# Rounded copies of the first two head pairs moved from GpSimd to ScalarE, and the last conditional laid out the other way round

## The chip, the cores and the metric

The kernel runs on one core of a Trainium2 chip. TensorE (PE; its weight loads are listed as PEld) multiplies matrices, VectorE (DVE), ScalarE (ACT) and GpSimd (POOL) work on tiles, and SyncE (SP) issues most of the DMA transfers; ACT and POOL issue some too. Every engine runs its own queue of instructions in order and waits on semaphores. The metric is the device time of one execution in microseconds (us); a change is judged against runs of the kernel before on the same chip.

## What is computed

Attention with a threshold, then a mixture of experts, then a second mixture whose experts are causal attentions:

```python
scores = scale * np.matmul(q, k.transpose(0, 1, 3, 2))          # 4 x 8 heads, 576 x 576
thresh = np.max(scores, axis=-1, keepdims=True) - tau
scores = np.where(scores >= thresh, scores, -1000000000.0)
scores = scores - np.max(scores, axis=-1, keepdims=True)
attn = np.exp(scores)
attn = attn / (np.sum(attn, axis=-1, keepdims=True) + 1e-09)
out = np.matmul(attn, v)
...
x = _moe_ref(x=x, **moe_kwargs)          # each token through one of 8 experts
return _moe2_ref(x=x, **moe2_kwargs)     # 4 causal attention experts, top 2 per token
```

## The kernel before

The kernel has three stages. Stage 1 (`stage1`) is the thresholded attention: 32 heads in 16 pairs (p = 0 to 15), each pair in 9 tiles of 128 rows of queries (j = 0 to 8: tiles 0 to 7 alternate between the two heads, a = j mod 2; tile 8 holds the last 64 rows of both). Stage 2 (`moe`) sends tokens through experts, stage 3 (`stage3`) is the second mixture. Almost all work of this change lies in the first 30 us and the last 20 us.

**Accuracy by splitting.** Scores are wanted with more precision than one pass of TensorE on rounded operands gives. So keys and queries are split: a rounded copy (`KK` of the keys times -0.125, `QS` of the queries) and the difference that rounding left (`KL`; for the queries the difference is written over the other 64 partitions of `QS`). `scores` (L242) multiplies `QS` with `KK` and with `KL`.

**Who splits.** `split_k` makes the rounded copy of the keys in two pieces (columns 0 to 575 for head 0, 640 columns for head 1): ScalarE for pair 0 (L191), GpSimd for every later pair (L189). `split_kl` makes the difference: VectorE for pair 0 (L200), GpSimd later (L202 scales the raw keys in place, L203 subtracts). Queries of pairs from 1 on come as a transfer that rounds (`split_q`, issued by GpSimd, L194), and `split_ql` makes the differences (GpSimd, L208). Queries of pair 0 are split by `split_q0` in three pieces of columns `QC` (128, 128 and 320 of each head): a cast (L212) and two subtractions (L215), by VectorE for piece 0 and by GpSimd for pieces 1 and 2. `merge` (L219) and `mixed` (L224, L225) gather operands for tile 8.

**The rest of a tile.** `rowmax` (DVE, L253) takes the extreme of a tile of scores, `thresh` (L258) adds tau, `expo` (ACT, L263) the exponential, `keep` (DVE, L276) applies the threshold; `tp` (PE, L289) transposes, `tp_ev` (ACT, L300, L302) brings the result back to SBUF, `av` (PE, L332) multiplies with the values. The scores rotate through three PSUM buffers (`tag="S", bufs=3`): the scores of a tile start only when `keep` of the tile three before has freed its buffer.

**What sets the order.** The order of stage 1 is written out by hand. `at(g, f, ...)` files a call under a due time g, one unit being a ninth of a pair (tile j of pair p has times 9p + W[name][j]); `E.run()` sorts by due time and then by order of filing, and the instructions go into the engines' queues in that order. Within a queue nothing overtakes.

**The end.** L1806 is a conditional (`tc.If`) around the work for experts whose tokens did not fit into the planned number of columns. It is not entered with these inputs. `preferred_fallthrough_block=False` puts the block for "not entered" straight behind the branch, with the long block "entered" behind it and the closing code (L1873: a barrier of all engines, clearing of semaphores) behind that. The block for "not entered" holds only waits; SP's wait there for the landing of the last transfers.

Of the kernel before, what the change touches and what calls it, by code (L numbers as in the profile page):

```python
# [14 lines left out]
AF = mybir.ActivationFunctionType  # L15
# [24 lines left out]
class Events:  # L40
# [4 lines left out]
    def at(self, g, pri, f, *a):  # L45
        self.n += 1
        self.ev.setdefault(g, []).append((pri, self.n, f, a))
# [67 lines left out]
def stage1(tc, nc, K, qT, qx, kT, vp, tau, wgl, x_dram, L, X, E2, hooks=(), npair=NP):  # L115
# [16 lines left out]
    QS = [E2.tile([128, 2, S], F32R, name=f"QS{i}", tag="w2h", bufs=4) for i in range(NQ)]  # L132
# [19 lines left out]
    Q0, QC = [], (slice(0, 128), slice(128, 256), slice(256, S))  # L152

    def load(p):
        if p:
            qr[p] = P1.tile([128, S], F32, name="qraw", bufs=2)
        kr[p] = P1.tile([128, 1216], F32, name="kraw", bufs=2)
        vr[p] = P1.tile([128, 640], F32, name="v", bufs=2)
        if p == 0:
            Q0.append(P1.tile([128, 2, S], F32, name="q0", tag="P", bufs=5))  # L160
            for i in range(2):
                nc.scalar.dma_start(Q0[0][:, :, QC[i]], qT[p][:, :, QC[i]])
            nc.sync.dma_start(kr[p][:, KC[0]], kT[p][:, KC[0]])
            nc.sync.dma_start(kr[p][:, KC[1]], kT[p][:, KC[1]])
            nc.sync.dma_start(taut, tau)
            nc.sync.dma_start(Q0[0][:, :, QC[2]], qT[p][:, :, QC[2]])
            K.load()
        else:
            nc.sync.dma_start(kr[p], kT[p])
            nc.sync.dma_start(qr[p], qx[p])  # L170
# [12 lines left out]
    def half(a):  # L183
        return slice(64 * a, 64 * a + 64)

    def split_k(p, a):
        o, r = KK[p % NK][:, KC[a]], kr[p][:, KC[a]]
        if p:
            nc.gpsimd.tensor_scalar(o, r, -0.125, 1.0, op0=ALU.mult, op1=ALU.mult)  # L189
        else:  # L190
            nc.scalar.activation(o, r, AF.Copy, scale=-0.125)  # L191
# [17 lines left out]

    def split_q0(k):  # L210
        eng, c = nc.gpsimd if k else nc.vector, QC[k]
        eng.tensor_copy(QS[0][:, :, c], Q0[0][:, :, c])  # L212
        for a in range(2):
            o = QS[0][half(1 - a), a, c]
            eng.tensor_sub(o, Q0[0][half(1 - a), a, c], o.bitcast(F32))  # L215
# [217 lines left out]
    at = lambda g, f, *a: E.at(g, 7, f, *a)  # L433
    for p in range(npair):
        g = 9 * p
        at(g - (27 if p < 2 else 21), load, p)
        at(g - (18 if p < 2 else 4.5), load_v, p)
        if p:
            at(g - (17 if p > 1 else 14.4), split_q, p)
        for a in range(2):  # L440
            if p:
                at(g - 9 + 2 * a, split_k, p, a)
                at(g - 8 + 2 * a, split_kl, p, a)
                at(g - 5 + a, split_ql, p, a)
            else:
                at(2 * a - 7, split_k, p, a)
                at(2 * a - 6, split_kl, p, a)
        if p == 0:
            for k, u in enumerate((-6.5, -5.5, -5.3)):
                at(u, split_q0, k)  # L450
            at(6, prep)
        at(g - 3.5, merge, p)
        if p < NMIX:
            at(g - 1.6, mixed, p)
        for j in range(9):
            for n, f in (("S", scores), ("red", rowmax), ("tau", thresh), ("exp", expo), ("keep", keep), ("tp", tp), ("ev", tp_ev)):
                at(g + W[n][j], f, p, j)
        at(g + W["diag"], diag, p)
        T = W
        if p == npair - 1:  # L460
            T = dict(W, row=(11.3, 14.36), rev=(11.7, 14.7), recip=10.6)
            at(g + 14.72, norm_last)
            at(g + 14.71, logits_last)
            at(g + 14.75, norm_last)
        for h in range(2):
            at(g + T["tpm"][h], tpm, p, h)
            at(g + T["pmev"][h], tpm_ev, p, h)
            for k in range(5):
                at(g + T["av"][h], av, p, h, k)
            at(g + T["xt"][h], av_ev, p, h)  # L470
            at(g + T["row"][h], rows, p, h)
            at(g + T["rev"][h], rows_ev, p, h)
        at(g + T["keep"][8] + 0.1, sums, p)
        at(g + T["recip"], recip, p)
        if p < npair - 1:
            at(g + T["rev"][1] + 0.1, norm, p)
# [14 lines left out]
    for g, f in hooks:  # L491
        g, late = g if isinstance(g, tuple) else (g, None)
# [408 lines left out]
class Weights:  # L901
# [9 lines left out]
    def more(self, pool, *ids):  # L911
        for i in ids:
            self.raw[i] = pool.tile([128, 2048], F32, name=f"raw{i}")
# [782 lines left out]
def model(tc, cst, qT, qx, kT, vp, tau, wgl, w12, wqk, wv, wo, out):  # L1696
    nc = tc.nc
    with ExitStack() as ctx:
# [6 lines left out]
        with ExitStack() as mx, ExitStack() as rx:  # L1705
# [4 lines left out]
            M = Box()  # L1710
# [38 lines left out]
            hooks = [(27, lambda *_: R.clear(tc)), *zip(EARLY, rt.early()), (W0, weights0), (R0, rows0)]  # L1749
            hooks += [*zip(TX0, (tx0(0), tx0(1))), *zip(S0, map(split0, (0, 1, 2, 3, 4, 6)))]  # L1750
            stage1(tc, nc, K, qT, qx, kT, vp, tau, wgl, x_dram, L, X, E, hooks)
            R.more(mx.enter_context(tc.tile_pool(name="mr", bufs=1)), 4, 5)
            W = mx.enter_context(tc.tile_pool(name="mo", bufs=1))
# [27 lines left out]
            def fetch3(b, j, i=None):  # L1781
                xr[b, j] = R.row(i)
                nc.gpsimd.indirect_dma_start(out=xr[b, j], out_offset=None, in_=yg,  # L1783
                                             in_offset=bass.IndirectOffsetOnAxis(ap=rt.slot[:, 4 * j + b:4 * j + b + 1], axis=0))

            def xscale(b, j):
                x = xr[b, j]
                eng = nc.gpsimd if b or j == 4 else nc.vector
                eng.tensor_scalar(x, x, rt.psel[:, 4 * j + b:4 * j + b + 1], 1.0, op0=ALU.mult, op1=ALU.mult)
# [13 lines left out]
        done = stage3(tc, nc, K, ws, xr, fetch3, xscale, R.row, out)  # L1803

        f = 2 * (PMAX + LMAX)
        with tc.If(nc.values_load(M.erow[0:1, f:f + 1], min_val=0, max_val=1) > 0, preferred_fallthrough_block=False):  # L1806
            with ExitStack() as rest, tc.manual_schedule():
                more(tc, nc, K, R, M, yg, rest)
            for j in range(4):
                fetch3(0, j, j)  # L1810
                xscale(0, j)
            stage3(tc, nc, K, ws, xr, fetch3, xscale, R.row, out, done)
# [64 lines left out]
```

## Time and profile before

| | |
|---|---|
| time before, median of 3 runs | 770.5 us (767.13 to 770.83) |
| profiled execution, its own time | 769.05 us |
| its span in the trace | 767.2 us |
| busy PE / DVE / ACT / POOL, share of the span | 95% / 71% / 64% / 38% |
| POOL busy, 20 to 40 us | 18.34 of 20 us |
| last instruction of the program proper (ACT L1626) | starts at 758.24 us |

The 1.85 us between the time and the span lie around the traced program. A profile of one execution gives each instruction a start, a duration and, where its engine stood idle before it, what ended the idle time. "Busy" of PE is modelled from the starts of the matmuls, so gaps under a matmul's length do not show as idle. POOL's shares are an average over three stages: it works mostly in the first.

### The profile page before, as it was taken

What the parts mean: (1) busy time and instruction counts of PE and PEld (TensorE: products, weight loads), DVE (VectorE), ACT (ScalarE), POOL (GpSimd) and SP (SyncE); (2) the same over time, 40 slices, a digit from 0 to 9 for tenths busy, and PEclk for the clock granted to TensorE, in tenths of its full rate; (3) what the DMA queues carried; (4) which work ended last, traced back from release to release, by engine and by line L of the source; (5) the groups of instructions that cost most, each with busy time, mean ns of one, the idle gap of its engine ahead of it and who ended that gap; (6) DMA issues with size and microseconds to landing.
All of it is one profiled execution on the core that took longest, in us unless ns stands there. A gap on an engine that the chain in (4) does not pass through costs nothing.

```text
span 767.2 us, 14238 instructions
## 1 busy us (share of the span) xinstructions
PE 732.3 (95%) x5076; PEld 619.5 (81%) x5076; DVE 547.8 (71%) x1423; ACT 488.4 (64%) x1019; POOL 288.3 (38%) x438
## 2 busy tenths in 40 slices
PE   5899999999998998999999999999989999999994
PEld 4787878887876677897899799989778888888873
DVE  7898998999998888613655465554268888978870
ACT  4788887888886684224554464544245887777872
POOL 6988888788777880300110010000383000000000
PEclk9999999999999899899999999999999999999998
DMA  7449443434341520484556656601241000100112
GB/s 250 150 131 311 138 143 127 158 119 128 113 143 34 237 59 18 131 323 167 203 206 236 231 164 212 241 1 52 93 124 56 2 15 1 42 15 29 42 42 86
DMA packets 37408, 95.40 MB, mean 124 GB/s; under 512 B 4336, under 2 KB 14832, under 8 KB 33232
## 3 DMA queue, kind: packets, MB, share of 16 engines
q1 hardware_dynamic: 30688, 73.49, 28.0%
q0 software_dynamic: 5360, 19.34, 8.0%
q10 hardware_dynamic: 1280, 1.57, 0.7%
q8 instruction: 42, 0.69, 0.4%
q14 instruction: 38, 0.31, 0.1%
HBM read 75.58 MB, written 18.81 MB: 123 GB/s over the span
## 4 chain that ended last, share of the span: by engine, by line
PE 53%; ACT 2%; DVE 2%; POOL 1%; issue 1%; ACTq 0%; POOLq 0%
PE py L1029 15%; PE acc L1004 15%; PE AV L1583 3%; PE X L1532 3%; PE misc L1345 1%; PE S L1462 1%; PE S L1463 1%; PE misc L1347 1%; PE misc L1346 1%; PE misc L1382 1%; PE misc L1384 1%; PE misc L1383 1%; PE misc L1614 1%; PE px L973 1%; PE misc L1613 1%
## 5 line engine op out<-in xcount | busy, mean ns | idle before, releaser
L276 DVE SCALAR_TENSOR_TENSOR P<-S,nm,E 128x576 f32<-128x576 f32 x144 | 116.1, 815 | 9.8 <-ACT E L263 3.8
L253 DVE TENSOR_REDUCE nm<-S 128x1 f32<-128x576 f32 x144 | 106.1, 753 | 19.5 <-PE S L242 18.6
L263 ACT ACTIVATE E<-S,nm 128x576 f32<-128x576 f32 x144 | 104.0, 747 | 9.8 <-DVE nm L253 9.1
L242 PE MATMUL S<-KK,QS 128*128 128x288 f32 x256 | 84.0, 343 | 11.2 <-DVE QS L215 5.7
L289 PE MATMUL X<-cst,P 128*128 128x128 f32 x576 | 86.9, 279 | 1.0 <-ACT PT L300 0.5
L1714 POOL DMA_INDIRECT xg<-x_dram,inv x22 | 22.9, 1042 | 166.9 <-PE px L973 151.0
L289 PEld LDWEIGHTS X<-cst,P 128*128 128x128 f32 x576 | 67.2, 142 | 16.5 <-issue 7.2
L300 ACT ACTIVATE PT<-X 128x512 f32<-128x512 f32 x128 | 75.6, 605 | 5.0 <-PE X L289 2.4
L1004 PE MATMUL acc<-xTh,w1l 128*128 128x256 f32 (+2 forms) x256 | 76.7, 300 | 0.0
L1004 PE MATMUL acc<-xTh,w1h 128*128 128x256 f32 (+2 forms) x256 | 76.6, 299 | 0.0
L1004 PE MATMUL acc<-xTl,w1h 128*128 128x256 f32 (+2 forms) x256 | 76.4, 298 | 0.0
L242 PE MATMUL S<-KL,QS 128*128 128x288 f32 x256 | 73.3, 300 | 0.3 <-DVE KL L200 0.3
L996 DVE SCALAR_TENSOR_TENSOR hTl<-acc,hTh 128x352 fp32r<-128x352 f32 (+2 forms) x52 | 30.0, 576 | 59.8 <-ACT hTh L995 59.8
L332 PE MATMUL Y<-PT,v 128*64 128x320 f32 (+1 forms) x512 | 71.3, 422 | 0.9 <-ACT PT L300 0.7
L1029 PE MATMUL py<-w2h,hTh 128*128 128x512 f32 (+2 forms) x176 | 71.1, 404 | 0.0
L1029 PE MATMUL py<-w2l,hTh 128*128 128x512 f32 (+2 forms) x176 | 69.6, 395 | 0.0
L1029 PE MATMUL py<-w2h,hTl 128*128 128x512 f32 (+2 forms) x176 | 69.3, 394 | 0.0
L995 ACT ACTIVATE hTh<-acc 128x352 fp32r<-128x352 f32 (+2 forms) x52 | 26.5, 509 | 63.3 <-PE acc L1004 63.3
L242 PEld LDWEIGHTS S<-KK,QS 128*128 128x128 f32 x256 | 49.6, 194 | 12.9 <-issue 6.0
L332 PEld LDWEIGHTS Y<-PT,v 128*64 128x64 f32 x512 | 34.5, 139 | 26.4 <-issue 6.8
L1783 POOL DMA_INDIRECT raw<-yg,slot x18 | 17.6, 981 | 95.8 <-DMA yg<-y 62.4
L242 PEld LDWEIGHTS S<-KL,QS 128*128 128x128 f32 x256 | 49.9, 195 | 0.6 <-DVE KL L200 0.6
(381 smaller groups left out, 2001.5 us busy)
## 6 DMA issues: line engine op xcount, KB each, us to landing
raw<-in_w_dram SPq DMA_DIRECT2D x32, 1024.0 KB, 5.4
kraw<-in_kT_dram SPq DMA_DIRECT2D x15, 608.0 KB, 4.1
QS<-in_qT_dram POOLq DMA_DIRECT2D x15, 576.0 KB, 4.0
v<-in_vp_dram SPq DMA_DIRECT2D x16, 320.0 KB, 2.9
yg<-y SPq DMA_DIRECT2D x17, 256.0 KB, 5.5
qraw<-in_qx_dram SPq DMA_DIRECT2D x15, 288.0 KB, 2.9
x_dram<-xr SPq DMA_DIRECT2D x16, 256.0 KB, 2.4
yg<-raw SPq DMA_DIRECT2D x1, 3072.0 KB, 13.0
```

What stands on the lines that cost most here:

```text
L242: nc.tensor.matmul(o, QS[p % NQ][:, a, cs], k[i][:, sl(576 * a)], start=(n == 0), stop=(n == 1))
L253: nc.vector.tensor_reduce(nm[:, 0:1], t[:, :, :288], axis=AX.XY, op=ALU.min)
L263: nc.scalar.activation(e, t[:, :, :288], AF.Exp, scale=-1.0, bias=nm[:, 0:1])
L276: nc.vector.scalar_tensor_tensor(PP[p, c][:, S * a:S * a + S].rearrange("p (h n) -> p h n", h=2), t[:, :, :288], nm[:, 1:2], e, op0=ALU.is ...
L289: nc.tensor.transpose(x[:, 128 * kc:128 * kc + 128], pp[:, o:o + 128], ident)
L300: nc.scalar.activation(PT[p, h][:, a, :, f:f + 128], x.rearrange("p (k q) -> p k q", k=4), AF.Copy)
L332: nc.tensor.matmul(out, l, r, start=s, stop=e, skip_group_check=True)
L995: nc.scalar.activation(hh, p, AF.Relu)
L996: nc.vector.scalar_tensor_tensor(hl, p, 0.0, hh.bitcast(F32), op0=ALU.max, op1=ALU.subtract)
L1004: nc.tensor.matmul(o, a[:, fs], x[:, k, 0:w], start=(first and n == 0), stop=(k == 3 and n == 2), skip_group_check=True)
L1029: nc.tensor.matmul(ys[t][u][0:m], h, w[:, 512 * f:512 * f + 512], start=(i == 0 and f == 0 and n == 0), stop=(i == 3 and f == 1 and n == 2))
L1532: nc.tensor.transpose(x[:, 128 * k:128 * k + 128], e[:, 128 * k:128 * k + 128], ident)
```

## The change

Nothing of the arithmetic changes, only who does it and when.

- Queries of pair 0: for pieces 1 and 2 the cast of `split_q0` moves from GpSimd to ScalarE; GpSimd keeps the two subtractions. Piece 1 is due at -4.5 (was -5.5), piece 2 at 0.95 (was -5.3), which is between the exponentials of tiles 0 and 1 in ScalarE's queue.
- The transfer of piece 1 of these queries is issued by SP behind the two of the keys, no longer by ScalarE.
- Keys of pair 1: the rounded copies (`split_k`) move from GpSimd to ScalarE, due 3.45 and 4.05: in its queue behind the exponentials of tiles 2 and 3. The differences follow at 3.5 and 4.1, so that GpSimd's order for pair 1 becomes: keys 0, queries 0, keys 1, queries 1 (it was keys 0, keys 1, queries 0, queries 1).
- `merge` and `mixed` of pair 0 are due at 1.2 and 1.3 (were -3.5 and -1.6), behind GpSimd's issue of `split_q(2)` (due 1.0).
- The last conditional gets `preferred_fallthrough_block=True`: the block "entered" comes straight behind the branch, the block for "not entered" behind it, next to the closing code.

```diff
             Q0.append(P1.tile([128, 2, S], F32, name="q0", tag="P", bufs=5))
-            for i in range(2):
-                nc.scalar.dma_start(Q0[0][:, :, QC[i]], qT[p][:, :, QC[i]])
+            nc.scalar.dma_start(Q0[0][:, :, QC[0]], qT[p][:, :, QC[0]])
             nc.sync.dma_start(kr[p][:, KC[0]], kT[p][:, KC[0]])
             nc.sync.dma_start(kr[p][:, KC[1]], kT[p][:, KC[1]])
+            nc.sync.dma_start(Q0[0][:, :, QC[1]], qT[p][:, :, QC[1]])
...
         o, r = KK[p % NK][:, KC[a]], kr[p][:, KC[a]]
-        if p:
+        if p > 1:
             nc.gpsimd.tensor_scalar(o, r, -0.125, 1.0, op0=ALU.mult, op1=ALU.mult)
         else:
             nc.scalar.activation(o, r, AF.Copy, scale=-0.125)
...
-        eng.tensor_copy(QS[0][:, :, c], Q0[0][:, :, c])
+        if k:
+            nc.scalar.activation(QS[0][:, :, c], Q0[0][:, :, c], AF.Copy)
+        else:
+            eng.tensor_copy(QS[0][:, :, c], Q0[0][:, :, c])
...
-            at(g - (17 if p > 1 else 14.4), split_q, p)
+            at(g - (17 if p > 1 else 13.4), split_q, p)
         for a in range(2):
             if p:
-                at(g - 9 + 2 * a, split_k, p, a)
-                at(g - 8 + 2 * a, split_kl, p, a)
+                at(g - 9 + 2 * a if p > 1 else 3.45 + 0.6 * a, split_k, p, a)
+                at(g - 8 + 2 * a if p > 1 else 3.5 + 0.6 * a, split_kl, p, a)
...
-            for k, u in enumerate((-6.5, -5.5, -5.3)):
+            for k, u in enumerate((-6.5, -4.5, 0.95)):
                 at(u, split_q0, k)
             at(6, prep)
-        at(g - 3.5, merge, p)
+        at(g - 3.5 if p else 1.2, merge, p)
         if p < NMIX:
-            at(g - 1.6, mixed, p)
+            at(g - 1.6 if p else 1.3, mixed, p)
...
-        with tc.If(nc.values_load(M.erow[0:1, f:f + 1], min_val=0, max_val=1) > 0, preferred_fallthrough_block=False):
+        with tc.If(nc.values_load(M.erow[0:1, f:f + 1], min_val=0, max_val=1) > 0, preferred_fallthrough_block=True):
```

## Rows read from the trace of the kernel before

**Rows 1.** Busy time by stretch: PE, PEld, DVE, ACT, POOL; PE's clock; DMA.

```profile
20.00:40.00 20.00, 17.91 (x141) 14.63 (x140) 16.52 (x43) 14.86 (x29) 18.34 (x32) 1.00 0.47 146
...
200.00:220.00 20.00, 20.00 (x162) 17.09 (x161) 18.16 (x47) 17.13 (x34) 13.39 (x21) 1.00 0.48 156
```

**Rows 2.** PE in order of time: start, duration, line, tiles, [idle before, releaser].

```profile
22.39 0.40 PE L242 MATMUL S<-KK,QS 128*128 128x288 f32 x1 [1.63 <-POOL QS L208]
...
23.87 0.40 PE L242 MATMUL S<-KK,QS 128*128 128x288 f32 x1 [0.46 <-POOL QS L208]
```

**Rows 3.** POOL in order of time, columns as in rows 2.

```profile
6.19 1.35 POOL L212 CAST QS<-q 128x256 fp32r<-128x256 f32 x1 [4.85 <-DMA q<-in_qT_dram]
...
9.34 0.72 POOL L212 CAST QS<-q 128x640 fp32r<-128x640 f32 x1
10.15 1.80 POOL L215 TENSOR_TENSOR QS<-q,QS 64x320 fp32r<-64x320 f32 x2
...
14.11 0.68 POOL L189 TENSOR_SCALAR KK<-kraw 128x576 fp32r<-128x576 f32 x1
...
15.63 1.43 POOL L203 TENSOR_TENSOR KL<-kraw,KK 128x576 fp32r<-128x576 f32 x1
16.99 0.59 POOL L194 DMA_DIRECT2D QS<-in_qT_dram  x1
17.61 0.74 POOL L189 TENSOR_SCALAR KK<-kraw 128x640 fp32r<-128x640 f32 x1
...
20.92 2.90 POOL L208 TENSOR_TENSOR QS<-qraw,QS 64x576 fp32r<-64x576 f32 x2
```

**Rows 4.** ACT in order of time, columns as in rows 2.

```profile
5.19 0.74 ACT L191 ACTIVATE KK<-kraw 128x640 fp32r<-128x640 f32 x1 [0.85 <-DMA kraw<-in_kT_dram]
8.52 0.74 ACT L263 ACTIVATE E<-S,nm 128x576 f32<-128x576 f32 x1 [2.59 <-DVE nm L253]
...
12.31 0.74 ACT L263 ACTIVATE E<-S,nm 128x576 f32<-128x576 f32 x1 [2.09 <-DVE nm L253]
13.94 0.60 ACT L300 ACTIVATE PT<-X 128x512 f32<-128x512 f32 x1 [0.89 <-PE X L289]
14.44 1.37 ACT L263 ACTIVATE E<-S,nm 128x576 f32<-128x576 f32 x2
```

**Rows 5.** DVE in order of time, columns as in rows 2.

```profile
15.95 0.81 DVE L276 SCALAR_TENSOR_TENSOR P<-S,nm,E 128x576 f32<-128x576 f32 x1
...
24.70 0.76 DVE L253 TENSOR_REDUCE nm<-S 128x1 f32<-128x576 f32 x1 [0.72 <-PE S L242]
```

**Rows 6.** SP's issues of transfers in order of time, columns as in rows 2.

```profile
3.58 0.43 SPq L173 DMA_DIRECT2D v<-in_vp_dram  x1
5.00 0.57 SPq L175 DMA_DIRECT2D iq<-in_wgl_dram  x1
```

**Rows 7.** Two transfers issued at 6.27 and 8.38: size, us from issue to landing.

```profile
kraw<-in_kT_dram SPq DMA_DIRECT2D x1, 608.0 KB, 5.9
...
qraw<-in_qx_dram SPq DMA_DIRECT2D x1, 288.0 KB, 9.0
```

**Rows 8.** Line L1806, the conditional: count, ns min/median/max, first and last start.

```profile
L1806 SPq EVENT_SEMAPHORE  x9: 17/17/17, 748.2 to 762.5; - x9
...
L1806 SPq COMPARE_BRANCH  x2: 38/48/57, 748.1 to 762.6; - x2
...
L1806 PEldq COMPARE_BRANCH  x2: 95/2157/4219, 754.8 to 757.9; - x2
...
L1806 ACTq COMPARE_BRANCH  x2: 38/43/48, 759.8 to 760.0; - x2
```

**Rows 9.** Line L1873, the closing code, columns as in rows 8.

```profile
L1873 SPq EVENT_SEMAPHORE  x14: 17/28/28, 765.5 to 767.1; - x14
...
L1873 ACTq DRAIN  x2: 8/46/83, 762.6 to 766.6; - x2
```

**Rows 10.** Busy time and clock in a stretch at half clock, columns as in rows 1.

```profile
250.00:253.00 3.00, 2.31 (x10) 1.00 (x10) 2.79 (x13) 1.86 (x3) 2.75 (x3) 0.51 0.00 0
```

## The prediction

> **What bounds the kernel now.** I read the busy time by stretch first. In stage 1's steady part PE is busy for all of 20 us (200 to 220), DVE for 18.2 and POOL for 13.4; between 20 and 40 us PE lacks 2.1 us and POOL has 18.3 [rows 1]. So what PE loses while the pipeline fills is lost for good, for nothing later has room to catch up, and what it gains there stays. PE's order of time then shows where it stands before the first scores of pair 1: 1.63 us at 22.39 and 0.46 us at 23.87, both until POOL's query differences [rows 2]. POOL's order of time shows why: from 6.19 on it works almost without a gap, and what PE waits for comes last, from 20.92 on, two instructions of 1.45 us [rows 3]. At the other end I read the two lines of the conditional and of the closing code. SP's last wait for a landing is over at 762.5, it branches at 762.6, and its next instruction starts at 765.5: 2.9 us after a branch that itself takes 38 ns [rows 8, 9]. ACT shows the same, branch at 760.0 and closing code at 762.6, and for PE the branch at 757.9 is itself recorded with 4.22 us. The first branch of each engine, which is not taken, is followed at once (SP: branch at 748.1, first wait at 748.2) [rows 8]. A taken jump over the long block thus costs 2.6 to 4.2 us, and SP pays it last, when everybody waits for it.
>
> **The front, step by step (times of the trace before in brackets).** POOL loses two casts, 1.35 and 0.72 us, and two copies of keys, 0.68 and 0.74: 3.5 us [rows 3]. ACT gains four copies. The copies of 640 columns and of 576 cost what ACT pays for pair 0, 0.74 and about 0.68 [rows 4]; 256 columns lie between nothing and those 0.74; I take 0.4, in proportion with a fixed part.
> - Query piece 1: it lands at about 6.2 as before (POOL's wait for it ends at 6.19 [rows 3]); ACT is free (its copy of keys ends at 5.93 [rows 4]), so POOL's subtractions start near 6.65 [7.64], a gain of 1.0 for the transfer of pair 1's queries that POOL issues behind them.
> - Query piece 2: ACT copies it behind the first exponential (8.52 + 0.74 [rows 4]) until 10.0. POOL's two subtractions start as before at 10.1 [10.15] and end at 11.9. The second exponential is queued behind the copy, starts near 10.05 and ends 0.1 us after VectorE is ready for it: 0.1 us, which the wait for the fourth exponential takes up again.
> - POOL then issues the transfer of pair 2's queries (0.59 us [rows 3]; was at 16.99), which pushes merge and mixed by 0.6 to an end at 14.7; tile 8 reads them after 19 us, so that is free. The transfer now goes out at 12 beside those of pair 2's keys, which POOL reads only after 25 us: free too.
> - Key differences of pair 1, head 0: from 14.7, as long as before (14.79 to 17.06, 2.3 us [rows 3]) until about 16.9. Query differences of head 0 follow at once, 1.45 us, until 18.3 [22.37]; keys of head 1 (18.35 to 20.92 before, 2.6 us) until 20.9; query differences of head 1 until 22.3 [23.82].
> - What it costs: ACT's copy of key piece 0 sits in the idle 0.89 us between the third exponential (ends 13.05) and the next work at 13.94 [rows 4], so it is free as long as the keys are there by 13.0. They were issued at 6.27 and took 5.9 us, 12.2 [rows 7]. SP now also issues query piece 1 (ACT took some 0.65 us for it), but SP stands idle from 4.01 to 5.00 [rows 6], so that later issues don't move. Copy of piece 1 has no such gap: it stands between the fourth and the fifth exponential (14.44, two in 1.37 [rows 4]) and delays the fifth by 0.74; DVE's keep of that tile (15.95 [rows 5]) slips to 16.6, and since DVE has no idle from there to the end of pair 0's last maximum, all of pair 0 slips by 0.67.
> - Result: PE's last transposes of pair 0 end at 21.4 instead of 20.76 (22.39 - 1.63 [rows 2]). The scores of pair 1 no longer wait for POOL but come at about 21.5 [22.39] and, when DVE has freed the buffer, at 22.65 [23.87]: PE is 1.2 us ahead. DVE gets the second tile at 23.95 [24.70, after 0.72 idle, rows 5], 0.75 ahead; it has enough slack in pair 1 to follow PE. **Front: -1.2 us**, carried to the end because PE is full. Bounds: -2.1 (both waits for POOL gone, nothing lost to the 0.67) and +0.7 (the slip, and no wait removed).
>
> **The end.** With the block for "not entered" next to the closing code each engine jumps at its first branch: SP at 748.1, 14 us before its last landing at 762.5; PE at 754.8, so at 759.1 with the 4.22 us of its own row; ACT at 759.8, 2.6 us, 762.4, hardly earlier than now (762.6) [rows 8, 9]. SP falls from its last wait (762.5) into the closing code, which takes 765.5 to 767.2 as before. **End: -2.9 us**; what is late next is ACT, at 762.5, and it has 0.8 us in hand, for SP runs through a dozen waits before the barrier. Bounds: 0 (a second jump remains) and -2.9.
>
> **The sum.** 769.05 of the profiled execution (span 767.2, 1.85 around it) - 1.2 - 2.9 = 764.95. That execution lies 1.45 under the median of the three runs; the spread is 767.13 to 770.83. I take the middle between the two, 769.8, as the base: 765.7.
>
> **The rivals.**
> - *The keys come late.* ACT's copy of key piece 0 waits at the head of its queue, and behind it the transposes' eviction and the exponential that VectorE needs. Every microsecond of landing after 13.0 costs one. For it: the transfer of pair 1's queries now starts 1 us earlier and shares the DMA engines with the keys. Against: 12.2 leaves 0.8. At 14.2 the front is worth nothing: 769.8 - 2.9 = 766.9.
> - *The same, to the other side.* If the keys' issue is also held up (transfers wait for older ones: SP stood until 5.00) and the landing takes 9 us as the slowest neighbour did [rows 7], 8.0 + 9 = 17 eats all 4.1; from a landing of 17.1 on the kernel is slower, at 18 by 0.9: 770.7. Against: 3 us of issue delay are nowhere in sight.
> - *The jump stays.* The block for "not entered" may still end in a jump for which SP waits 2.9 us, or SP's early jump is undone by something else last: only the front is left, 768.6. For it: it ends in a jump now. Against: its target then stands right behind it. [...]
> [...]
>
> **How the numbers follow.** Forecast 0.62, late keys 0.16, late keys and slower 0.05, jump stays 0.08, a clock stretch less 0.07, one more 0.02. A measurement of this kernel tells about 0.5% (3.85 us) from no change, and the forecast of 4.1 lies close to that: two thirds of its 0.62 count as faster (0.41), the rest as same. Faster 0.41 + 0.07 = 0.48; same 0.21 + 0.16 + 0.08 + 0.02 = 0.47; slower 0.05. The range 763.0 to 769.2 holds the forecast with the spread of the runs, the late keys and the stubborn jump, and leaves out the clock's gift and the slower case.
>
> **What would show it.** Right: ACT copies near 6.2, 9.3, 13.1 and 15.1; no L212 and L189 of POOL before 25 us; PE's waits for POOL L208 gone and the second scores of pair 1 near 22.7; the pause of 2.6 to 4.2 us behind each engine's first branch, and SP's closing code 0.1 us behind its last landing. Wrong: ACT standing for a DMA at 13; PE still standing before pair 1; a pause between SP's last landing and L1873; later pairs of tiles less far ahead than pair 1, which would mean that PE did not bound the fill.

## The result and the profile after

The changed kernel takes 762.53 us (median of five, 762.1 to 763.7) against 770.5 us (767.13 to 771.67). The ratio is 0.9912 [0.9894, 0.9931]: 6.8 us less, with an interval of 5.3 to 8.2. (The two medians lie 8.0 us apart; gains in this document go by the ratios and their intervals.) The forecast was 765.7, 4.1 us less than its base, and the range began at 763.0; the measured median lies half a microsecond below it, and 770.5 x 0.9912 = 763.7 lies inside. The sign and the two places were right, and each place gave more than it was priced at. The profiled execution of after took 762.1 us, span 760.3.

| | before | after |
|---|---|---|
| first scores of pair 0 (PE), us | 5.71 | 4.84 |
| first scores of pair 1 (PE), us | 22.39 | 20.71 |
| first rows of pair 0 evicted (ACT, line 344, now 347), us | 27.46 | 25.44 |
| from ACT's last output transfer to SP's last wait, us | 3.65 | 3.15 |
| from SP's last wait to SP's closing code, us | 2.98 | 0.07 |

**The front.** Here are PE, ACT, POOL and DVE of after in order of time (lines past the edit have moved by 3):

```profile
20.71 0.37 PE L245 MATMUL S<-KK,QS 128*128 128x288 f32 x1
...
21.88 0.37 PE L245 MATMUL S<-KK,QS 128*128 128x288 f32 x1 [0.18 <-DVE P L279]
```
```profile
5.91 0.40 ACT L213 ACTIVATE QS<-q 128x256 fp32r<-128x256 f32 x1
...
8.29 0.73 ACT L213 ACTIVATE QS<-q 128x640 fp32r<-128x640 f32 x1
...
12.30 0.67 ACT L191 ACTIVATE KK<-kraw 128x576 fp32r<-128x576 f32 x1
...
14.42 0.74 ACT L191 ACTIVATE KK<-kraw 128x640 fp32r<-128x640 f32 x1
...
25.44 0.38 ACT L347 ACTIVATE XT<-Y 128x256 f32<-128x256 f32 x1 [0.45 <-PE Y L335]
```
```profile
15.89 1.44 POOL L208 TENSOR_TENSOR QS<-qraw,QS 64x576 fp32r<-64x576 f32 x1
...
19.75 1.42 POOL L208 TENSOR_TENSOR QS<-qraw,QS 64x576 fp32r<-64x576 f32 x1
```
```profile
4.08 0.29 DVE L215 CAST QS<-q 128x256 fp32r<-128x256 f32 x1 [1.88 <-DMA q<-in_qT_dram]
...
14.56 0.82 DVE L279 SCALAR_TENSOR_TENSOR P<-S,nm,E 128x576 f32<-128x576 f32 x1 [0.38 <-ACT E L266]
...
15.82 0.82 DVE L279 SCALAR_TENSOR_TENSOR P<-S,nm,E 128x576 f32<-128x576 f32 x1 [0.43 <-ACT E L266]
```

POOL's last query difference ends at 21.17 [rows 3: 23.82], and PE's waits for it, 1.63 and 0.46 us [rows 2], are gone; the second scores of pair 1 now wait 0.18 us for DVE. ACT's four copies are there at the durations expected, and none of them waits for a transfer. DVE's cast at 4.08 shows one thing that was not expected: the first queries land 0.87 us earlier than in the profiled execution of before, so pair 0 starts earlier by as much.

**The middle.** Between 28 us and the end of the second stage the lead over before grows from 2.0 to 3.3 us, in one place: the half-clock stretch of before [rows 10] is missing. The window of after, then that of the same front with before's closing layout (e2 below):

```profile
250.00:253.00 3.00, 3.00 (x24) 1.81 (x19) 2.94 (x11) 1.04 (x2) 2.85 (x3) 1.00 0.37 85
```
```profile
250.00:253.00 3.00, 3.00 (x14) 1.36 (x13) 2.93 (x12) 0.42 (x1) 2.81 (x2) 0.55 0.28 44
```

**The end.** The conditional and the closing code of after (count, ns min/median/max, first and last start):

```profile
L1809 SPq EVENT_SEMAPHORE  x9: 17/17/17, 747.8 to 758.6; - x9
...
L1809 SPq COMPARE_BRANCH  x1: 53/53/53, 744.8 to 744.8; - x1
...
L1809 PEldq COMPARE_BRANCH  x1: 3482/3482/3482, 751.4 to 751.4; - x1
...
L1809 ACTq COMPARE_BRANCH  x1: 54/54/54, 756.4 to 756.4; - x1
```
```profile
L1876 SPq EVENT_SEMAPHORE  x14: 17/28/28, 758.7 to 760.2; - x14
...
L1876 ACTq DRAIN  x2: 8/8/8, 759.2 to 759.8; - x2
```

Each engine now branches once. SP pays its jump at 744.8 (next instruction at 747.8) while the outputs are still being made, and goes from its last wait (758.6) into the closing code (758.7); before, 2.9 us lay between [rows 8, 9].

### The profile page after: what moved, and what is told of

Same layout as the page of the kernel before. It is cut to its first block, busy times and chain, and to the rows that moved or that the text cites. A ratio compares the mean times of both kernels' runs of the same rounds, so it can differ in the third digit from the quotient of the medians.

```text
span 760.3 us, 14234 instructions
## 1 busy us (share of the span) xinstructions
PE 730.5 (96%) x5076; PEld 618.5 (81%) x5076; DVE 546.9 (72%) x1423; ACT 490.7 (65%) x1023; POOL 284.8 (37%) x434
## 4 chain that ended last, share of the span: by engine, by line
PE 54%; DVE 2%; ACT 2%; POOL 1%; issue 1%; ACTq 0%; POOLq 0%
PE py L1032 15%; PE acc L1007 15%; PE AV L1586 3%; PE X L1535 3%; PE misc L1348 1%; PE S L1465 1%; PE S L1466 1%; PE misc L1350 1%; PE misc L1349 1%; PE misc L1385 1%; PE misc L1387 1%; PE misc L1386 1%; PE misc L1617 1%; PE px L976 1%; PE misc L1616 1%
## 5 line engine op out<-in xcount | busy, mean ns | idle before, releaser
L335 PE MATMUL Y<-PT,v 128*64 128x320 f32 (+1 forms) x512 | 69.1, 412 | 0.9 <-ACT PT L303 0.7
L998 ACT ACTIVATE hTh<-acc 128x352 fp32r<-128x352 f32 (+2 forms) x52 | 26.5, 509 | 63.3 <-PE acc L1007 63.3
```

The lines of the kernel that those rows point to most:

```text
L335: nc.tensor.matmul(out, l, r, start=s, stop=e, skip_group_check=True)
L998: nc.scalar.activation(hh, p, AF.Relu)
```

## The experiments

Each ratio is against the kernel before, measured beside it on the same chip. The table holds what the traces show at the two disputed places. "Rows" is ScalarE's first eviction of pair 0's rows, the last column the time from ACT's last output transfer to the end of the span.

| kernel | ratio and interval | PE's waits for POOL before pair 1's first, second scores | rows | PE's clock, 24 to 26, 26 to 28 us | transfer to end |
|---|---|---|---|---|---|
| before | | 1.63, 0.46 | 27.46 | 1.00, 1.00 | 8.3 |
| after | 0.9912 [0.9894, 0.9931] | none | 25.44 | 1.00, 1.00 | 4.8 |
| e1 layout only | 0.9955 [0.9937, 0.9973] | 2.22, 0.49 | 30.04 | 0.72, 0.50 | 4.8 |
| e2 front only | 0.9957 [0.9941, 0.9972] | none | 25.97 | 1.00, 1.00 | 8.4 |
| e3 one transfer | 0.9980 [0.9962, 0.9999] | 2.13, 0.48 | 29.71 | 0.50, 0.50 | 8.7 |
| e4 transfer put back | 0.9909 [0.9875, 0.9942] | none | 25.96 | 1.00, 1.00 | 4.9 |
| e5 keys only | 0.9908 [0.9877, 0.9939] | none | 25.40 | 1.00, 1.00 | 4.8 |
| e6 queries only | 0.9957 [0.9939, 0.9975] | none, 1.79 | 26.65 | 1.00, 1.00 | 4.9 |
| e7 later copy | 0.9913 [0.9896, 0.9931] | none, 0.25 | 25.14 | 1.00, 1.00 | 4.9 |
| e8 no block | 0.9891 [0.9870, 0.9911] | none | 25.15 | 1.00, 1.00 | 2.9 |
| f1 filled wait | 0.9974 [0.9962, 0.9986] | 0.42, 0.48 | 28.40 | 1.00, 1.00 | 8.2 |
| f2 wait put back | 0.9941 [0.9921, 0.9962] | 2.80, none | 28.27 | 1.00, 1.00 | 5.1 |
| f3 put back, filled | 0.9938 [0.9914, 0.9963] | 0.70, none | 28.19 | 1.00, 1.00 | 5.0 |
| f4 layout, filled wait | 0.9941 [0.9918, 0.9965] | none, 0.49 | 26.96 | 1.00, 1.00 | 5.0 |

**Which part brings what.** e1 takes the kernel before with the new layout alone, e2 the changed kernel with the old layout.

```diff
-preferred_fallthrough_block=False
+preferred_fallthrough_block=True
```

> The kernel before with the conditional laid out the other way round and nothing else. Theory A (the jump is worth its 2.9 us and the last landing was held up besides, by the code that PE loads at that time): the span ends 3.4 us earlier counted from the last ScalarE instruction, some 766.5 us against 770. Theory B (only the jump, the 0.5 us of the last landing are chance): 2.9 us, and the last transfer takes 3.6 us to land as before. In both the front shows pair 1's second scores at 23.9 us as before. Rival (the end gains nothing, all came from elsewhere): time as before.

> The changed kernel with the conditional as before: only the front. Expected: pair 1's second scores at 21.9 us as in the changed kernel (before 23.9), a gain of 2.0 us that holds through stage 1, SP's 2.9 us between its last landing and the closing code back. Time: 2.0 us under before if the rest of the changed kernel's gain (1.2 us lost or won between 245 and 260 us, where PE ran at half clock before and did not after) is chance; 3.3 us under before in every run if the front's shift itself does away with that stretch. The granted clock of the runs tells: 0.986 with it, 0.992 without, in the runs of the changed kernel.

The layout is worth 0.45% (3.5 us), the front 0.43% (3.3 us), and 0.9955 x 0.9957 = 0.9912: the parts add up. In e1's trace the time from the last transfer to the end is 3.5 us shorter than in before (4.8 against 8.3): 2.9 of it is the jump, 0.5 the last landing (3.12 against 3.65 us), as in theory A; its reason, the code that PE loads, is not tested by this run. Its front missed what was expected: pair 1's second scores come at 24.89, not at 23.9; why stands below. e2 gains the 3.3 us and not the 2.0, and yet the half-clock stretch at 250 us stands in its trace, so neither of its two cases holds as it was put; its second scores come at 22.41, not at 21.9, for its first queries land as late as before's. The end was forecast at 2.9 and the front at 1.2, so most of what is missing from the forecast is missing from the front.

e8 is the changed kernel without the block for "not entered".

> The changed kernel without the conditional and its block at the end, so that no engine jumps (the work for experts whose tokens don't fit is left out; it is not entered with these inputs). If the jump is hidden in the changed kernel (every engine's jump ends before SP's last landing or within what SP still does), the closing code starts no earlier after the last landing and the time is the changed kernel's less at most 0.1 us. If ScalarE's jump still counts, up to 0.6 us less. If code loads slow the last landing, it takes 2.7 us or less instead of 3.1.

It is 0.9891, some 1.6 us under the changed kernel, though the intervals overlap. Its trace ends 1.9 us sooner after the last transfer (2.9 against 4.8). The transfer is seen 2.0 us after its issue (755.78 to 757.82) instead of 3.15, and SP's part of the closing code behind that takes 0.9 us instead of 1.6 (compare the row of after's L1876 above):

```profile
L1867 SPq EVENT_SEMAPHORE  x12: 17/28/28, 745.1 to 758.7; - x12
```

So what the conditional still costs in this trace is 1.1 us in the last landing and 0.8 in the closing code; the expectation had at most 0.6 us of time and a landing of 2.7 or less.

**Was it the transfer?** The first queries land 0.87 us earlier in after, and the change takes the transfer of piece 1 off ACT's queue. e3 moves only that transfer in the kernel before; e4 puts it back in the changed one.

```diff
-            for i in range(2):
-                nc.scalar.dma_start(Q0[0][:, :, QC[i]], qT[p][:, :, QC[i]])
+            nc.scalar.dma_start(Q0[0][:, :, QC[0]], qT[p][:, :, QC[0]])
...
+            nc.sync.dma_start(Q0[0][:, :, QC[1]], qT[p][:, :, QC[1]])
```

> The kernel before, with only the transfer of query piece 1 moved from ScalarE's queue to SP's, behind the keys. Theory: behind piece 0 in the same queue it holds up the landing of piece 0 by 0.87 us; so the first scores come at 4.84 instead of 5.71 us, but GpSimd's chain still sets the start of pair 1, and only its own earlier start (piece 1 lands a little earlier) is left there: second scores of pair 1 0.2 to 0.5 us earlier than 23.87, time 0.2 to 0.5 us under before. Rival (the landing was early by chance, or by another part of the change): first scores at 5.71.

> The changed kernel with that one transfer put back into ScalarE's queue. Theory: first scores back at 5.7 us, all of pair 0 0.87 us later, second scores of pair 1 at 22.7 us: this is what the forecast had (22.65), and the front is worth 1.2 us against before instead of 2.0. Rival: first scores stay at 4.84, and the front at 2.0.

In the changed kernel the transfer's new place is not needed: e4 is as fast, within an interval of 0.3% to either side. In the kernel before it may help: e3 is 0.20% faster, 1.5 us [0.1, 2.9], where 0.2 to 0.5 us were expected. The landing of piece 0 scatters by itself. With piece 1 behind piece 0 on ACT's queue VectorE's first cast starts at 4.95 (before), 4.82 (e4), and 4.04 in e1, whose front is that of before, instruction for instruction:

```profile
4.04 0.29 DVE L212 CAST QS<-q 128x256 fp32r<-128x256 f32 x1 [1.85 <-DMA q<-in_qT_dram]
```

With piece 1 on SP's queue it starts at 4.08 (after), 4.21 (e3), 4.83 (e2). So the 0.87 us by which the first queries land earlier in after than in before is chance.

Piece 1 scatters too. Behind piece 0 on ACT's queue the wait for it ends at 6.19 (before), 6.00 (e4) and 5.57 (f4), but at 8.23 in e1 and 8.07 in f1, both with before's front. Here is POOL in e1, its first cast and its last query differences:

```profile
8.23 0.40 POOL L212 CAST QS<-q 128x256 fp32r<-128x256 f32 x1 [6.90 <-DMA q<-in_qT_dram]
...
21.93 2.90 POOL L208 TENSOR_TENSOR QS<-qraw,QS 64x576 fp32r<-64x576 f32 x2
```

POOL's chain then ends at 24.83 and 24.76 instead of 23.82 [rows 3], and pair 1's scores come up to 1.0 us later than in the trace of before. On SP's queue the piece was there by 5.99 in all nine traces. How often it is late on ACT's queue, and whether e3's gain is this, no run shows.

**Which copies?** e5 leaves the casts of pair 0's queries on POOL, e6 the copies of pair 1's keys.

```diff
-        if k:
-            nc.scalar.activation(QS[0][:, :, c], Q0[0][:, :, c], AF.Copy)
-        else:
-            eng.tensor_copy(QS[0][:, :, c], Q0[0][:, :, c])
+        eng.tensor_copy(QS[0][:, :, c], Q0[0][:, :, c])
```
```diff
-        if p > 1:
+        if p:
             nc.gpsimd.tensor_scalar(o, r, -0.125, 1.0, op0=ALU.mult, op1=ALU.mult)
```

> The changed kernel with the casts of pair 0's queries left on GpSimd (cast and two subtractions, at the new places): only the keys' copies and the transfer have moved. GpSimd's chain is 0.7 us longer than in the changed kernel, second query differences ready near 22.0 us instead of 21.2, just when VectorE frees the buffer: second scores of pair 1 at 21.9 to 22.1, time as the changed kernel within 0.2 us. Theory: the queries' copies are worth next to nothing by themselves. Rival: they carry the front, and 1 us or more is lost.

> The changed kernel with the keys' rounded copies of pair 1 left on GpSimd (at the new places): GpSimd's chain is 1.6 us longer, second query differences ready near 22.8 us, while VectorE is 0.67 us earlier for want of the copy before the fifth exponential. Second scores of pair 1 at 22.8 instead of 21.9, time 0.8 us over the changed kernel. Rival (the copies are worth nothing, since what GpSimd saves ScalarE loses): 21.9 and no difference.

The key copies are the whole front that these runs can tell: e5 equals the changed kernel, and e6, which keeps the transfer, the new order of POOL and the query copies, equals e1. In e6 PE still stands 1.79 us for POOL, before the second scores of pair 1:

```profile
23.05 0.40 PE L245 MATMUL S<-KK,QS 128*128 128x288 f32 x1 [1.79 <-POOL QS L208]
```

e6 was expected 0.8 us over the changed kernel and lies 3.8 us over e5 (0.9957 against 0.9908, in the same set of runs). Its trace shows 1.25 of that at the rows (26.65 against 25.40); another 2.0 come behind 244 us (span 763.3 against 760.0), with the half-clock stretch at 250 us, which e5's trace lacks.

e7 gives ACT the copy of the second key piece after the fifth exponential, so that it no longer delays that exponential; POOL's work that needs the copy is filed behind it.

```diff
-at(g - 9 + 2 * a if p > 1 else 3.45 + 0.6 * a, split_k, p, a)
+at(g - 9 + 2 * a if p > 1 else (3.45, 5.53)[a], split_k, p, a)
...
```

> The changed kernel with ScalarE's copy of the second key piece moved from between the exponentials of tiles 3 and 4 to behind the eviction of tile 1, where ScalarE stands idle for 1.1 us before the exponential of tile 5; GpSimd's second key difference and what follows it are filed behind it, in the same order. If the copy in front of the fifth exponential cost pair 0 what the forecast said (0.67 us on VectorE and with it on PE), the second scores of pair 1 come at 21.2 instead of 21.9 us and the kernel is 0.6 us faster than the changed one. Rival: GpSimd is late next and nothing moves (second scores at 21.9).

In its trace the rows come 0.3 us earlier than in after, though its first queries landed 0.35 us later; the second scores come at 21.56, not at 21.2, behind 0.25 us of waiting for POOL. Its time is the same: a gain of that size isn't seen in five runs.

**Why the front is worth 3.3 us.** The traces of e1 and e3 hold a part of the answer. POOL's work before pair 1 is that of before in both, and yet their rows come 2.6 and 2.2 us later than in the trace of before:

```profile
25.03 1.95 PE L332 MATMUL Y<-PT,v 128*64 128x256 f32 x16
```
```profile
27.46 0.38 ACT L344 ACTIVATE XT<-Y 128x256 f32<-128x256 f32 x1 [0.46 <-PE Y L332]
```

In e1 1.0 us of this is POOL's late start; in e3 POOL's chain even ends 0.7 us earlier (23.09). But PE waits longer than the 1.63 us of before (e1, then e3; start, duration, [wait]), and behind the wait its clock is halved:

```profile
23.38 0.40 PE L242 MATMUL S<-KK,QS 128*128 128x288 f32 x1 [2.22 <-POOL QS L208]
...
27.00 2.56 PE L332 MATMUL Y<-PT,v 128*64 128x256 f32 x16
```
```profile
21.64 0.40 PE L242 MATMUL S<-KK,QS 128*128 128x288 f32 x1 [2.13 <-POOL QS L208]
...
25.25 3.68 PE L332 MATMUL Y<-PT,v 128*64 128x256 f32 x16
```

Windows of e1, then e3 (columns as in rows 1):

```profile
24.00:26.00 2.00, 1.51 (x8) 1.27 (x7) 0.76 (x1) 1.02 (x2) 2.00 (x7) 0.72 0.46 172
26.00:28.00 2.00, 2.00 (x11) 1.27 (x12) 1.56 (x3) 0.89 (x2) 1.96 (x6) 0.50 0.44 134
```
```profile
24.00:26.00 2.00, 2.00 (x10) 1.44 (x11) 1.30 (x3) 0.64 (x2) 1.96 (x7) 0.50 0.58 148
26.00:28.00 2.00, 2.00 (x12) 1.08 (x10) 1.78 (x7) 1.22 (x2) 1.69 (x6) 0.50 0.05 12
```

The 16 matmuls that take 1.95 us in before and after take 2.56 and 3.68. From PE's first scores of pair 1 to the rows it is 5.07 us in before (27.46 - 22.39), 6.66 in e1 and 8.07 in e3: 1.6 and 3.0 us go to the clock. The profiled execution of before did not have this stretch: its clock stands at 1.00 from 22 to 30 us. To see what it costs on the mean, f1 gives PE twelve matmuls to do while it stands there, and changes nothing else; f4 is f1 with the new layout.

```diff
         t = PS.tile([128, 2, 512], F32, name="S", tag="S", bufs=3)
+        if (p, j) == (1, 0):
+            for n in range(12):
+                nc.tensor.matmul(t[:, 0, :288], QS[0][:, 0, 0:128], KK[0][:, 0:288], start=True, stop=True)
```

> The kernel before, with twelve more matmuls in front of the first scores of pair 1 (pair 0's operands, into the same accumulator, which the real scores then overwrite): 12 x 0.13 = 1.6 us of work for PE while it stands there for POOL; nothing else is changed. Theory 'the wait brings the half clock': behind the longer of these waits (2.1 and 2.2 us in the two runs with this front) PE ran at 0.50 for 4 to 6 us, and 2.0 us were lost; with PE at work no stretch below 1.00 stands in 20 to 30 us, the first eviction of pair 0's rows (ScalarE, line 344 in the kernel before) lies at 26.5 to 27.5 and not near 29.8, and the time is on the mean 1 to 2 us under the kernel before (ratio 0.9975 to 0.9985). Rival 'the stretch comes by chance, whatever PE does': it still appears in most runs, ratio 1.000. Rival 'the dummies delay the real scores': ratio 1.001 or more, the first scores of pair 1 later than POOL's last query difference by more than 0.1 us.

> The kernel before with the conditional laid out the other way round and with the twelve added matmuls ahead of the first scores of pair 1; copies, order and transfers of the front as before. If the gain of the whole change is the end (3.5 us in the traces with this layout), plus a half-clock stretch that PE's wait in the front brings in most executions (2.0 us by the run with the added matmuls alone), plus some 1.4 us by which pair 1's scores come earlier, then this kernel holds the first two: ratio 0.9955 x 0.9974 = 0.993 (764.9 on 770.3), 1.4 us over the changed kernel (0.9912), and its runs scatter less than those of the kernel before. Rival 'the copies on ScalarE bring all of the front, the clock nothing': as with the layout alone, 0.9955. Rival 'the added matmuls already bring all of the front': 0.9912.

f1 is 0.26% [0.14, 0.38] faster than before, 2.0 us, though PE does more and no data comes earlier. Its trace (the added matmuls; the scores behind them; the rows; a window):

```profile
21.04 1.85 PE L234 MATMUL S<-KK,QS 128*128 128x288 f32 x12
...
23.31 0.40 PE L245 MATMUL S<-KK,QS 128*128 128x288 f32 x1 [0.42 <-POOL QS L208]
...
25.97 1.95 PE L335 MATMUL Y<-PT,v 128*64 128x256 f32 x16
```
```profile
26.00:28.00 2.00, 2.00 (x21) 1.32 (x20) 1.70 (x6) 1.86 (x3) 1.96 (x6) 1.00 0.42 133
```

The clock stands at 1.00. The rows come at 28.40, outside the 26.5 to 27.5 expected, because query piece 1 landed late (POOL began at 8.07); from the first scores to the rows it is 5.09 us, as in before. Over all runs the mean granted clock is 0.9874 in f1 (12 runs) and 0.9846 in the 18 runs of before beside them; the difference, over 767 us, is 2.1 us of PE's time by estimate. The times spread over 2.2 us (766.92 to 769.12) instead of 4.7 (767.53 to 772.25). That is what one stretch less in most executions would look like. The front alone agrees (e2, 0.9881 in 7 runs against 0.9847 in 12), but the mean clock of a few runs is not sharp: e1, with before's front, has 0.9865 in 6. f4 came out at 0.9941: the forecast product of 0.993 lies inside its interval, but so does e1's 0.9955, so it adds little; that the added matmuls bring all of the front is just outside (0.9912 against 0.9918). That its runs would scatter less came true: 3.1 us against 5.0, at a mean clock of 0.9907 against 0.9847.

The other direction failed. f2 puts a wait back into the changed kernel by making POOL late, f3 fills that wait.

```diff
     def split_ql(p, a):
         i = p % NQ
+        if (p, a) == (1, 0):
+            for _ in range(3):
+                r = kr[p][:, KC[0]]
+                nc.gpsimd.tensor_scalar(r, r, 1.0, 1.0, op0=ALU.mult, op1=ALU.mult)
...
-at(g - 5 + a, split_ql, p, a)
+at(g - 5 + a if (p, a) != (1, 0) else 5.05, split_ql, p, a)
```

> The changed kernel with the wait of PE put back: POOL works pair 1's second head first and then scales a slice of the keys that are used up by 1.0 three times (3 x 0.76 us) before it makes the query differences of the first head, so the first scores of pair 1 come near 23.4 instead of 20.7 and PE stands about 2.8 us before them. ScalarE's copies, the transfers and the end stay. Theory 'the wait brings the half clock': PE at 0.50 for some 5 us behind the wait, the 16 matmuls of the rows (128x256) take about 3.7 us instead of 1.95, pair 1 starts 2.0 to 2.7 us later by the wait and 2 us more by the clock: 4 to 5 us over the changed kernel, about 767. Rival 'a wait costs only itself': 2.0 to 2.7 us over it, about 765, clock 1.00.

> The kernel with POOL's query differences put late, and with sixteen more matmuls (2.1 us, pair 0's operands) for PE while it waits for them, as the only difference between the two. Theory 'the wait brings the half clock': PEclk 1.00 through 20 to 30 us, the 16 matmuls of the rows at 1.95 us, 2 us faster than the same kernel without the added matmuls: about 765, 2.0 to 2.7 us over the changed kernel. Rival 'a wait costs only itself': the same time as without them.

PE stands 2.80 us in f2, longer than in e1 and e3, and the clock does not fall behind it:

```profile
23.92 0.40 PE L249 MATMUL S<-KK,QS 128*128 128x288 f32 x1 [2.80 <-POOL QS L212]
...
25.85 1.95 PE L339 MATMUL Y<-PT,v 128*64 128x256 f32 x16
```
```profile
26.00:28.00 2.00, 2.00 (x20) 1.19 (x18) 1.70 (x6) 1.82 (x4) 1.87 (x5) 1.00 0.33 121
```

f2 and f3 take the same time (0.9941, 0.9938), as the rival has it, but with five and four runs and intervals of 0.2% to either side the 2 us in question could hide there. So f2's trace refutes that a long enough wait always halves the clock; how often one does behind this wait is not shown. f2 lies 0.29%, 2.2 us, over the changed kernel, which is what the wait itself would cost. What stays is narrower: behind this wait the clock fell in two of the three traces that hold before's front unfilled (before, e1, e3), and filling the wait made the kernel 2.0 us faster. That these 2.0 us are the clock's is borne out by the mean clock and the spread of the runs, not by a trace of before with and without the stretch. What else decides whether it falls is open.

## Why the prediction came out as it did

- **What bounds the kernel was read rightly.** What PE lost in the fill was lost for good: the lead that after has at its first rows (2.02 us) is still 2.1 at 244 us. Nothing gave it back.
- **The durations held.** 0.4 for the 256 columns (measured 0.40), 0.74 and 0.68 for the others (0.73, 0.67, 0.74). The slip by the copy of key piece 1 was set at 0.67: DVE's keep of the tile before starts 0.65 earlier than in before (14.56 against 15.21), this one 0.13 (15.82 against 15.95 [rows 5]), so it slipped by 0.52. Key pieces came in time (copy at 12.30 without a wait), and both rivals of late keys did not happen.
- **The chain of the front was sized about rightly, at 1.2 us.** Traces whose first queries landed as late as before's are e2 and e4 (first scores at 5.59 and 5.58 against 5.71). Their rows come 1.5 us earlier, 1.4 without those 0.12. Of the 2.02 in the trace of after, the other 0.5 goes with its earlier landing (rows at 25.44 against 25.97 and 25.96).
- **The step that failed is the base of the front.** That PE loses 1.63 and 0.46 us was read from one execution, and its lower bound of -2.1, both waits gone, was taken as the most that there was to gain. In two other traces of the same POOL work the wait was followed by half clock, at 1.6 and 3.0 us. Measured, the front is worth 3.3 us [2.2, 4.5]; 1.4 of it is the chain, and the 1.9 that are left agree with the 2.0 [1.1, 2.9] of f1. That all of the 1.9 is the clock is not shown: the late landing of query piece 1, up to 1.0 us in e1 and f1, is another loss of before's front that its profiled execution was spared. The prediction gave a clock stretch less a chance of 0.07 and one more 0.02 (the trace of before has one at 250 us [rows 10]); it did not ask whether the very wait that is removed brings one in executions other than the profiled one.
- **A clock stretch less came true in the trace, not as a cause.** The stretch at 250 us, at a clock of 0.51 in before [rows 10], is missing in after and worth 1.2 us there; how large the clock's gift is that the range leaves out, no run shows beyond that. But the same 1.6 us of idle stand ahead of it in all traces (1.56 to 1.59, PE waiting for DVE), and it follows in before, e1, e2, e6, e8, f1, f2 and f3 and not in after, e3, e4, e5, e7 and f4. It is a toss that one profile can't price; what decides it is not shown.
- **The end was 2.9 and measured 3.5.** The mechanism was right (a jump at the first branch of each engine, closing code 0.07 us behind SP's last landing, ACT not late). The term was mis-sized twice. In e2, e3 and f1 SP's pause behind its last branch is 3.2, 3.4 and 3.2 us; the 2.9 of the profiled execution was at the low end. And the last landing comes faster with the new layout: 3.07 to 3.39 us after its issue in the nine traces with it and with the block, 3.35 to 3.65 in the four without. Why is not shown; but between that transfer's issue and its landing the instruction queues (q8 and q14) moved three packets in each of the four, two in each of the nine and none in e8, which agrees with theory A.
- **"The jump stays"** fell with e1 alone: its time from the last transfer to the end is 3.5 us shorter than in before. What a branch costs depends on its way here: not taken, it is recorded with 57 ns (SP) and 95 (PE); behind SP's jump 2.9 us pass until its next instruction [rows 8, 9].

## What to carry to other kernels

Price a wait of TensorE not by its idle time alone: look in several traces whether its clock halves behind it, because one profiled execution may have been spared (here 1.00 behind 1.63 us in before, 0.50 behind 2.22 in e1); a few matmuls of no use in the wait are a three-line test (2.0 us in f1). Put the unlikely side of a conditional where the likely side needs no jump after the last transfer (here 2.98 us behind SP's last wait became 0.07). And before a difference of a microsecond at the start of two traces is explained, see how the same landing scatters in kernels whose start is identical (usable at 4.95 us in before, at 4.04 in e1).

## What the runs showed of the hardware

- The first transfer of 128 KB, issued at 0.73 or 0.74 us in all kernels, was usable at 4.02 to 4.95 us, whatever queue the second went to.
- The second piece of these queries, behind the first on ACT's queue, was usable at 5.57 to 6.19 us in three traces and at 8.07 and 8.23 in two; on SP's queue, behind the keys, by 5.99 in all nine.
- Starting earlier can cost: in e3 the first queries landed 0.74 us earlier than in before, PE was done with pair 0 by 19.51 instead of 20.76, waited 2.13 us for POOL instead of 1.63, and then ran at a clock of 0.50 (24 to 28 us); its rows came 2.25 us later.
- Behind a wait of 2.80 us PE's clock stayed at 1.00 (f2), behind waits of 2.13 and 2.22 it stood at 0.50 (e3 and e1, 26 to 28 us).
- In after the jump over the long block costs 2.6 to 3.5 us until the engine's next instruction (SP 744.8 to 747.8, ACT 756.4 to 759.0, PE 3.48 in the branch itself). Moved ahead of the last landing, it left 0.07 us between SP's last wait and the closing code.
- Without the block the last landing was seen 2.04 us after its issue (e8), with it 3.07 to 3.65 us.
